# Writing out TensorE's order for the layer change and the second attention: quarters of P times V between score pieces, P turned one unit ahead

## The chip, the cores and the metric

The kernel runs on one core of one Trainium2 chip. The metric is the device time of one execution in microseconds (us), given as the median of several executions. A ratio is the mean time of one kernel's fast runs over the mean time of the other kernel's fast runs of the same rounds, so it is not quite the ratio of the medians that stand beside it. The medians and ranges are over all runs of a kernel, those in the slow state too: one slow run each in e4, e10, e11 and e13, and three in e5. A verdict of faster or slower needs the 95% interval to lie outside 2%.

Two words are used throughout. TensorE is *warm* when its clock runs in full and *cold* when it runs at half rate. The Trainium skill, "TensorE: Matmul & The Clock Gate", Part 1, says that the half rate is the default and that a busy window of about 3.4 us (free-running) releases it. Traces agree on the two states: a score matmul of 512 columns takes 628 ns in one and about 400 ns in the other, with little in between. The clock column of the profile is not always right about the state, so in this text a state is read from those durations.

A *unit* is one key-value head of the attention: scores, softmax, P times V, output projection. There are 8 in each attention.

## The reference, cut to what matters

```python
def _A_ref(x, k_cache, v_cache, wq, wo):          # B=4, 1 query row, 32 heads on 8 kv heads, Dh=128
    W = min(4096, max(256, Sk // 4))              # Sk=8192: the last 2048 keys
    q = (x @ wq).reshape(B, Sq, Hq, Dh).transpose(0, 2, 1, 3)
    k = jnp.repeat(k_cache[:, :, Sk - W:, :], rep, axis=1)
    v = jnp.repeat(v_cache[:, :, Sk - W:, :], rep, axis=1)
    p = _softmax(jnp.einsum("bhqd,bhkd->bhqk", q, k) * (Dh ** -0.5), axis=-1)
    return jnp.einsum("bhqk,bhkd->bhqd", p, v)... @ wo

x = x + _A_ref(_layernorm(x), ...)                # first attention
x = x + _B_ref(_layernorm(x), ...)                # gated MLP
x = x + _A_ref(_layernorm(x), ...)                # second attention, same K, V and weights
x = x + _B_ref(_layernorm(x), ...)
```

## The kernel before

Operations are recorded with what they read and write. A list scheduler with a small time model then fixes the order of each engine, so the source order is only a priority. These are the parts that matter, for one unit.

```python
def softmax_unit(tag, hk):
    q_unit(tag, hk, k2)                                   # "qx" on TensorE, "qe": ACT copies to qbd
    def e_s(pe):                                          # ONE operation of 20 matmuls
        for gi in range(4): pe.matmul(ps[...bank...], msk_s, msk_m..., start=True, stop=False)       # L713, mask
        for cp in range(4):
            for gi in range(4): pe.matmul(ps[...], qbd[...], kt[...], start=False, stop=(cp == 3))   # L720, scores
    P.op("tensor", "S" + tag, ...)
    P.op("vector", "mx" + tag, ...)                       # L728 maximum, then three small steps to nm (L740)
    P.op("scalar", "ex" + tag, ...)                       # L743 exponential

def turn_p(tag, k2):
    P.op("tensor", "pp" + tag, ...)                       # L752 one 128x512 matmul
    P.op("scalar", "pc" + tag, ...)                       # L754 copy
    P.op("vector", "pt" + tag, ...)                       # L757 transpose to ebuf
    ...                                                   # four small POOL steps
    P.op("tensor", "sb" + tag, ...); P.op("vector", "ri" + tag, ...)   # L771, L778: 1/sum

def pv_unit(tag, h, k2, tiles):
    for bp, name in tiles:
        P.op("tensor", "PV...", 32 matmuls, ...)          # L792, twice 32 matmuls
    P.op("vector", "oe" + tag, ...)                       # L800 scaling by 1/sum
    P.op("tensor", "pm" + tag, ...); P.op("vector", "oq" + tag, ...)   # L810, L815

def attn(L):
    for ui in range(2):
        ks[ui] = front(ui); turn_p(ui)                    # front = scores and softmax
    for ui, h in enumerate(hs):
        if ui + 2 < HKV: ks[ui + 2] = front(ui + 2)
        ov = pv_unit(tag, h, ks[ui], v_tiles[(L, h)])
        if ui + 2 < HKV: turn_p(ui + 2)
        wo_unit(tag, h, ov, ...)                          # L831, 16 matmuls
    # ... (cut)

fill(); x_in()
q_proj(0, ...); attn(0); glu(0, 0, NB)
q_proj(1, ...); attn(2); glu(1, 0, NB, True)
```

Of the kernel before, what the change touches and what calls it, by code (L numbers as in the profile page):

```python
# [40 lines left out]
class _Plan:  # L41
    def __init__(self):
        self.ops = []
        self.last_w = {}
        self.readers = {}
        self.bank_eng = {}
        self.bank_cur = {}
        self.bank_prev = {}

    def op(self, eng, name, dur, emit, r=(), w=(), banks=(), dma_bytes=0, dma_rate=0.0, after=(), lazy=0.0):  # L50
# [26 lines left out]
        for t in w:  # L77
            self.last_w[t] = o
            self.readers[t] = []
        deps.discard(o)  # L80
# [168 lines left out]
class _SlotPool:  # L249
# [14 lines left out]
    sem_lat=100.0, pick_tol=60.0,  # L264
    dma_issue=60.0, dma_lat0=900.0, dma_lat1=1100.0, dma_max_out=16,
    bw_8k=430.0, bw_4k=412.0, bw_3k=409.0, bw_1k=356.0,
    pe_pair=38.0, pe_small=230.0, pe_f32=450.0, pe_row=80.0, pe_sq=300.0,
    dve_fix=150.0, dve_f32=1.04, dve_small=90.0,
# [4 lines left out]
def build(nc, A_x, A_k, A_v, A_wq, A_wo, B_wg, B_wu, B_wd, out, cfg=None):  # L273
# [41 lines left out]
    with es:  # L315
# [56 lines left out]
        def tile_ap(s):  # L372
            return arena[:, s * SLOT:(s + 2) * SLOT]
# [42 lines left out]
        def need(name):  # L416
            while name not in where:
                take_load()
            return where[name]
# [53 lines left out]
        def wq_part(k, c, i):  # L473

            if k == 0:
                return ("wq", c, k), i * SLOT
            return ("wq", (i, c // 2), k), (c % 2) * SLOT
# [161 lines left out]
        def q_proj(k, b0, b1, variance):  # L639
            assert b0 == 0 and b1 == NB  # L640
            after = ()
            for n, i in enumerate((0, 1) if k == 0 else (1, 0)):
                qb = OBS[n]
                for c in range(NC):
                    name, o = wq_part(k, c, i)
                    s = need(name)

                    def e_q(pe, c=c, s=s, qb=qb, o=o):
                        last = None
                        for hh in range(4):  # L650
                            last = pe.matmul(ps[32 * hh:32 * hh + NB, qb, :], xn[:, c * NB:(c + 1) * NB],  # L651
                                             tile_ap(s)[:, o + hh * 512:o + (hh + 1) * 512],
                                             start=(c == 0), stop=(c == NC - 1))
                        return last
                    P.op("tensor", "q%d_%d_%d" % (k, i, c), 4 * tm["pe_row"], e_q,
                         r=tok(s) + [("xn",)], w=[("qrow", i)], banks=(qb,), after=after if k else ())
                    done(name)
                if variance is not None:
                    variance()
                    variance = None  # L660
                P.op("vector", "qt%d_%d" % (k, i), c_dve(512),
                     lambda v, qb=qb: v.transpose(  # L662
                         ebuf[:, :], ps[:, qb, :].rearrange("p (x k t) -> p x t k", k=32, t=2)),
                     r=[("qrow", i)], w=[("e", 0), ("e", 1)], banks=(qb,))
                qi = qh[:, i * 64:(i + 1) * 64]
                qc = P.op("vector", "qc%d_%d" % (k, i), c_dve(64),
                     lambda v, qi=qi: v.tensor_tensor(
                         qi.rearrange("p (c b r) -> p c b r", c=4, b=NB),
                         ebuf[:, :].rearrange("p (r c y) -> p c y r", c=4, y=32)[:, :, 0:NB],
                         lnr[:, 0:NB].unsqueeze(1).unsqueeze(3).broadcast_to([128, 4, NB, REP]), ALU.mult),  # L670
                     r=[("e", 0), ("e", 1), ("lnr", 0)], w=[("qh", i)])
                if k and n == 0:
                    fresh.append(qc)
                    after = (qc,)
# [26 lines left out]
        ucount = [0]  # L701

        def softmax_unit(tag, hk):
# [4 lines left out]
            q_unit(tag, hk, k2)  # L708

            def e_s(pe):  # L710
                last = None
                for gi in range(4):
                    last = pe.matmul(ps[32 * gi:32 * gi + 32, bank, :], msk_s[:, :],  # L713
                                     msk_m[:, :].unsqueeze(1).broadcast_to([128, 256, 2]), start=True, stop=False)
                for cp in range(4):
                    for gi in range(4):
                        jh, bp = gi // 2, gi % 2
                        kt = kpair(hk, bp).rearrange("p (j c k t) -> p c t j k", c=2, k=32, t=2)
                        q0 = ((k2 * 4 + cp) * 2 + bp) * 32
                        last = pe.matmul(ps[32 * gi:32 * gi + 32, bank, :], qbd[:, q0:q0 + 32],  # L720
                                         kt[:, cp // 2, cp % 2, jh * NJ:(jh + 1) * NJ, :], start=False, stop=(cp == 3))
                return last
            P.op("tensor", "S" + tag, 20 * tm["pe_row"], e_s,
                 r=[("msk_s",), ("msk_m",)] + [("slot", 4 * hk + t) for t in range(4)] + [("q", k2)],
                 w=[("pss", pt)], banks=(bank,))
# [4 lines left out]
            for g in range(2):  # L730
# [8 lines left out]
            P.op("vector", "nm" + tag, tm["dve_small"],  # L739
                 lambda v: v.tensor_reduce(nmax[:, 2 + k2:3 + k2], mk, AXX, ALU.max, negate=True, apply_transpose=True),  # L740
# [6 lines left out]
            return k2  # L747

        def turn_p(tag, k2):
            ob = OBS[k2]  # L750
# [16 lines left out]

            def e_sb(pe):
                last = None
                for n, sn in enumerate((hi, mid, lo)):  # L770
                    last = pe.matmul(ps[:, ob, 128:128 + NR], sn.broadcast_to([128, 128]), sel_b[:, :],  # L771
                                     start=(n == 0), stop=(n == 2))
                return last
            P.op("tensor", "sb" + tag, 3 * tm["pe_pair"], e_sb,
                 r=[("s3", k2, n) for n in range(3)] + [("sel_b",)], w=[("psb", k2)], banks=(ob,))
            rv = rinv[:, k2 * NR:(k2 + 1) * NR]
            P.op("vector", "ri" + tag, c_dve(NR) + 60.0,
                 lambda v: v.reciprocal(rv, ps[:, ob, 128:128 + NR]),  # L778
                 r=[("psb", k2)], w=[("rinv", k2)], banks=(ob,))

        def pv_unit(tag, h, k2, tiles):
            ob = OBS[k2]
            ev = ebuf[:, k2 * 256:(k2 + 1) * 256].bitcast(BF16).rearrange("p (m x t) -> p t m x", x=32, t=2)
            for bp, name in tiles:
                s = need(name)

                def e_pv(pe, s=s, bp=bp):
                    last = None
                    src = tile_ap(s)
                    for j in range(2 * NJ):  # L790
                        x0 = j // 16 * 16 + bp * 8
                        last = pe.matmul(ps[:, ob, bp * 8:bp * 8 + 8], src[:, j * 128:(j + 1) * 128],  # L792
                                         ev[:, j % 2, j % 16 // 2, x0:x0 + 8], start=(j == 0), stop=(j == 2 * NJ - 1))
                    return last
                P.op("tensor", "PV%s_%d_%d" % (tag, h, bp), 2 * NJ * tm["pe_pair"], e_pv,
                     r=tok(s) + [("e", k2)], w=[("pso", k2, bp)], banks=(ob,))
                done(name)
            ov = onb[:, k2 * NR:(k2 + 1) * NR]
# [5 lines left out]
                 r=[("pso", k2, bp) for bp in range(2)] + [("rinv", k2)], w=[("on", k2)], banks=(ob,))  # L804
            op = onp[:, k2 * REP * NR:(k2 + 1) * REP * NR]
# [34 lines left out]
        def attn(L):  # L840
            hs = list(range(HKV)) if L == 0 else list(range(HKV))[::-1]

            def front(ui):
                h = hs[ui]
                if L == 0:
                    k_transpose(h)
                k2 = softmax_unit("%d.%d" % (L, ui), h)
                if L == 2:
                    for bp in range(2):
                        pool.release(4 * h + 2 * bp)  # L850
                    fill()
                return k2

            ks = {}
            for ui in range(2):
                ks[ui] = front(ui)
                turn_p("%d.%d" % (L, ui), ks[ui])
            for ui, h in enumerate(hs):
                tag = "%d.%d" % (L, ui)
                if ui + 2 < HKV:  # L860
                    ks[ui + 2] = front(ui + 2)
                if L == 0 and ui == HKV - 1:
                    stash(stashed)
                ov = pv_unit(tag, h, ks[ui], v_tiles[(L, h)])
                if ui + 2 < HKV:
                    turn_p("%d.%d" % (L, ui + 2), ks[ui + 2])
                wo_unit(tag, h, ov, ks[ui], ui == 0, ui == HKV - 1)
# [154 lines left out]
        q_proj(0, 0, NB, layer_norm("A", 0, NB, True))  # L1022
        attn(0)
        glu(0, 0, NB)
        q_proj(1, 0, NB, layer_norm("Q", 0, NB, True))
        attn(2)
# [70 lines left out]
```

## Time and profile before

| | before |
|---|---|
| time, median of 3 (range) | 188.27 us (188.03 to 188.72) |
| span in the profiled run | 186.5 us |
| bytes by DMA, end of the last load | 71.84 MB, about 178.9 us |
| first P times V of the second attention | 137.05 us |
| last output projection of the second attention ends | 175.47 us |
| from there to the end of the span | 11.0 us |

The span in 40 slices: each digit is the busy share of a slice in tenths, PEclk is the granted clock.

```profile
## 2 busy tenths in 40 slices
PE   1434433764716465352855473358778988995694
PEclk9999999999999999999999999999987555576558
DMA  5999999999999999999999999999899999999910
```

The DMA row is full until 177 us. The chain that ended last, as shares of the span, says the same: mostly memory stream.

```profile
DMA 47%; PE 25%; DVE 13%; SPq 6%; ACT 4%; issue 4%; ACTq 0%
```

The turn of P (L752) is missing among the matmuls of the timeline, and only its weight loads have a record:

```profile
157.27 0.10 PEld L752 LDWEIGHTS ps<-prow,perm 128*128 128x128 bf16 x1 [0.32 <-ACT prow L743]
162.87 0.10 PEld L752 LDWEIGHTS ps<-prow,perm 128*128 128x128 bf16 x1
```

The exponentials' line from the groups of 115 to 185 us (busy, mean ns, idle before, releasers) is the symptom that the change aims at:

```profile
L743 ACT ACTIVATE prow<-ps,nmax 128x512 bf16<-128x512 f32 x8 | 5.5, 688 | 18.7 <-DVE onb L800 12.8 <-DVE nmax L740 5.1 <-DVE ebuf L757 0.8
```

### The profile page before, as it was taken

To read this page: it belongs to the slowest core of one execution; us is meant where nothing else is said; L and a number is where in the kernel's file an instruction comes from. 1 tells how busy PE (TensorE), PEld (TensorE's weight loads), DVE (VectorE), ACT (ScalarE), POOL (GpSimd) and SP (SyncE) were. 2 spreads that over 40 slices of the span, in tenths; PEclk is the share of its full clock that TensorE was granted. 3 is DMA by queue.
4 is the path that set the end of the run, shared out by engine and by line. 5 is a ranking of instruction groups with operands and counts; after the bars stand their busy time and mean duration, and the time that the engine had idled before them with its cause. 6 is when DMAs were issued, how large, how long until landed. Compare 5 with 4: busy or idle time off the path is not lost.

```text
span 186.5 us, 4596 instructions
## 1 busy us (share of the span) xinstructions
PE 109.6 (59%) x2018; PEld 65.5 (35%) x2032; DVE 93.4 (50%) x240; ACT 31.1 (17%) x78; POOL 15.8 (9%) x85
## 2 busy tenths in 40 slices
PE   1434433764716465352855473358778988995694
PEld 1002111342403333141444431312255655655532
DVE  4209999376583737639242543216754413442241
ACT  2002003230212103020020010001263213212010
POOL 7000001110100001010010000000031111012000
PEclk9999999999999999999999999999987555576558
DMA  5999999999999999999999999999899999999910
GB/s 196 422 427 427 422 416 417 417 420 418 413 427 417 422 422 411 427 424 413 419 417 417 399 403 419 334 375 420 353 411 427 425 418 417 416 403 406 378 55 1
DMA packets 12307, 72.12 MB, mean 387 GB/s; under 512 B 1144, under 2 KB 1152, under 8 KB 5632
## 3 DMA queue, kind: packets, MB, share of 16 engines
q1 hardware_dynamic: 12280, 71.84, 94.4%
q8 instruction: 15, 0.25, 0.5%
q14 instruction: 4, 0.03, 0.0%
q10 hardware_dynamic: 8, 0.00, 0.0%
HBM read 71.83 MB, written 0.00 MB: 385 GB/s over the span
## 4 chain that ended last, share of the span: by engine, by line
DMA 47%; PE 25%; DVE 13%; SPq 6%; ACT 4%; issue 4%; ACTq 0%
DMA arena<-in_A_v_cache_dram 23%; DMA arena<-in_A_k_cache_dram 14%; PE ps L720 9%; SPq L387 6%; DMA arena<-in_A_wq_dram 5%; DMA arena<-in_B_w_up_dram 5%; PE ps L792 4%; DVE arena L698 3%; PE ps L713 3%; ACT prow L743 3%; PE ps L893 2%; DVE nmax L728 2%; PE ps L651 2%; DVE ps L496 1%; PE ps L831 1%
## 5 line engine op out<-in xcount | busy, mean ns | idle before, releaser
L792 PE MATMUL ps<-ebuf,arena 128*128 128x8 bf16 x1024 | 32.0, 168 | 23.1 <-DMA arena<-in_A_v_cache_dram 17.2
L792 PEld LDWEIGHTS ps<-ebuf,arena 128*128 128x128 bf16 x1024 | 29.9, 103 | 25.7 <-DMA arena<-in_A_v_cache_dram 22.1
L698 DVE STREAM_TRANSPOSE arena<-arena 128x1024 f32<-128x1024 f32 x32 | 37.9, 1213 | 1.1 <-DMA arena<-in_A_k_cache_dram 1.0
L720 PE MATMUL ps<-arena,qbd 128*32 128x512 bf16 x256 | 29.2, 595 | 0.0
L728 DVE TENSOR_REDUCE nmax<-ps 128x1 f32<-128x512 f32 x16 | 11.0, 687 | 26.1 <-PE ps L720 26.0
L713 PE MATMUL ps<-msk_m,msk_s 128*32 128x512 bf16 x64 | 10.1, 583 | 15.6 <-DVE arena L698 13.2
L743 ACT ACTIVATE prow<-ps,nmax 128x512 bf16<-128x512 f32 x16 | 11.0, 687 | 49.4 <-DVE nmax L740 25.1
L761 POOL CAST s<-psm 128x1 bf16<-128x1 f32 x16 | 3.0, 186 | 147.8 <-ACT prow L743 147.8
L651 PE MATMUL ps<-arena,xn 128*4 128x512 bf16 x64 | 8.4, 606 | 8.9 <-DMA arena<-in_A_wq_dram 7.8
L720 PEld LDWEIGHTS ps<-arena,qbd 128*32 128x32 bf16 x256 | 9.1, 132 | 12.2 <-issue 11.3
L691 ACT CAST qbd<-ps 128x256 bf16<-128x256 f32 x16 | 5.9, 371 | 38.1 <-PE ps L720 30.7
L754 ACT CAST prow<-ps 128x512 bf16<-128x512 f32 x16 | 9.4, 586 | 10.5 <-PE ps L810 3.2
L831 PE MATMUL ps<-onp,arena 128*128 128x16 bf16 x256 | 9.2, 174 | 3.0 <-DVE onp L815 3.0
L757 DVE STREAM_TRANSPOSE ebuf<-prow 128x256 f32<-128x256 f32 x16 | 6.9, 431 | 6.4 <-ACT prow L754 6.3
L800 DVE TENSOR_TENSOR onb<-ps,rinv 128x16 bf16<-128x16 f32 x16 | 2.8, 174 | 13.8 <-PE ps L792 13.8
L662 DVE STREAM_TRANSPOSE ebuf<-ps 128x512 f32<-128x512 f32 x4 | 2.9, 717 | 13.5 <-PE ps L651 13.4
L831 PEld LDWEIGHTS ps<-onp,arena 128*128 128x128 bf16 x256 | 8.0, 103 | 4.0 <-DVE onp L815 2.0
L628 ACT ACTIVATE lnv<-ps 128x4 f32<-128x4 f32 x4 | 0.7, 174 | 49.7 <-PE ps L624 49.7
L686 PE MATMUL ps<-qh,eyew 32*128 32x64 bf16 x64 | 5.9, 226 | 5.0 <-ACT qbd L691 1.9
L893 PE MATMUL ps<-arena,xn 128*4 128x448 bf16 x64 | 6.8, 564 | 2.4 <-DMA arena<-in_B_w_up_dram 1.7
L713 PEld LDWEIGHTS ps<-msk_m,msk_s 128*32 128x32 bf16 x64 | 1.9, 100 | 17.0 <-DVE arena L698 10.1
L810 PE MATMUL ps<-onb,permo 128*128 128x16 bf16 x64 | 4.3, 178 | 3.6 <-DVE onb L800 3.6
(75 smaller groups left out, 92.7 us busy)
## 6 DMA issues: line engine op xcount, KB each, us to landing
arena<-in_A_v_cache_dram SPq DMA_DIRECT2D x30, 1024.0 KB, 20.6
arena<-in_A_k_cache_dram SPq DMA_DIRECT2D x16, 1024.0 KB, 25.1
arena<-in_A_wq_dram SPq DMA_DIRECT2D x8, 1024.0 KB, 9.5
arena<-in_A_wo_dram SPq DMA_DIRECT2D x4, 1024.0 KB, 25.2
arena<-in_B_w_gate_dram SPq DMA_DIRECT2D x4, 896.0 KB, 17.7
arena<-in_B_w_up_dram SPq DMA_DIRECT2D x4, 896.0 KB, 15.9
arena<-in_B_w_down_dram SPq DMA_DIRECT2D x2, 1024.0 KB, 12.8
arena<-in_B_w_down_dram SPq DMA_DIRECT2D x1, 768.0 KB, 7.4
```

The source lines that it names most:

```text
L387: o = P.op("sync", name, 0.0, lambda e, dst=dst, src=src: e.dma_start(dst, src), r=r, w=w, dma_bytes=nbytes, dma_rate=tm[rate])
L651: last = pe.matmul(ps[32 * hh:32 * hh + NB, qb, :], xn[:, c * NB:(c + 1) * NB], tile_ap(s)[:, o + hh * 512:o + (hh + 1) * 512], start=(c = ...
L698: P.op("vector", "T%d_%d" % (h, t), c_dve(1024), lambda v, v32=v32: v.transpose(v32, v32), r=[("slot", 4 * h + t)], w=[("slot", 4 * h + t)])
L713: last = pe.matmul(ps[32 * gi:32 * gi + 32, bank, :], msk_s[:, :], msk_m[:, :].unsqueeze(1).broadcast_to([128, 256, 2]), start=True, stop= ...
L720: last = pe.matmul(ps[32 * gi:32 * gi + 32, bank, :], qbd[:, q0:q0 + 32], kt[:, cp // 2, cp % 2, jh * NJ:(jh + 1) * NJ, :], start=False, s ...
L728: lambda v: v.tensor_reduce(nmax[:, k2:k2 + 1], ps[:, bank, :], AXX, ALU.max),
L743: lambda a: a.activation(prow[:, :].rearrange("p (m x t) -> p m x t", x=32, t=2), ps[:, bank, :].rearrange("p (m t x) -> p m x t", x=32, t ...
L754: P.op("scalar", "pc" + tag, c_act(512), lambda a: a.copy(prow[:, :], ps[:, PBS[k2], :]), r=[("ppb", k2)], w=[("prow",)], banks=(PBS[k2],))
L757: lambda v: v.transpose(ebuf[:, k2 * 256:(k2 + 1) * 256], prow[:, :].bitcast(F32)),
L792: last = pe.matmul(ps[:, ob, bp * 8:bp * 8 + 8], src[:, j * 128:(j + 1) * 128], ev[:, j % 2, j % 16 // 2, x0:x0 + 8], start=(j == 0), stop ...
L831: last = pe.matmul(ps[:, WB, c * NR:(c + 1) * NR], tile_ap(s)[:, o + r_ * D + c * 128:o + r_ * D + (c + 1) * 128], ov[:, r_ * NR:(r_ + 1) ...
L893: last = pe.matmul(ps[32 * g:32 * g + NB, OBS[n], 0:NF], xn[:, c * NB:(c + 1) * NB], tile_ap(s)[:, o:o + NF], start=(c == 0), stop=(c == N ...
```

## The change

The intent is to break the loop of latencies. TensorE's order is no longer left to the scheduler from the second query projection to the end of the second attention: every TensorE operation depends on the one before it (`P.chain`). The score block of unit u+2 is split into five pieces, mask and four score pieces, which stand between quarters of unit u's P times V. P of unit u+1 is turned in the middle of unit u. Four 512-column matmuls a unit (`filler`) are added, meant to keep the clock up. A quarter of the second query projection (two of its eight groups of four matmuls) moves behind the first two score blocks. Constants of the scheduler's time model change too. The core of the diff:

```diff
+        if eng == "tensor":
+            if self.chain:
+                deps.add(self.last_t)
+            self.last_t = o
...
-        def softmax_unit(tag, hk):
+        def score_pieces(tag, hk):
+            def piece(cps, last):          # cps: (-1,) the mask, (0,) to (3,) four score matmuls each
...
+        def filler(k2):
+            def e_f(pe):
+                for g in range(4):
+                    last = pe.matmul(ps[32 * g:32 * g + 32, PBS[k2], :], permo[:, 32 * g:32 * g + 32], permo[:, :], start=True, stop=True)
...
+        def attn_second():
+            for u in range(2):
+                q_unit(tag(u), hs[u], u)
+                sp, soft_late = score_pieces(tag(u), hs[u])
+                sp((-1, 0, 1, 2, 3), u == 0)
+                free(u)
+            q_rest((nms[tag(0)],))
+            q_unit(tag(2), hs[2], 0)
+            turn_a(tag(0), 0)
+            turn_b(tag(0), 0)
+            soft_late()
+            for u in range(HKV):
...
+                pv(0)
+                score(-1)
+                score(0)
+                if u == HKV - 1:
+                    op[u - 1] = o_turn(tag(u - 1), 1 - k2)
+                pv(1)
+                if u < HKV - 1:
+                    project()              # output projection of unit u-1
+                score(1)
+                pv(2)
+                if u == HKV - 1:
+                    project()
+                else:
+                    turn_a(tag(u + 1), 1 - k2)
+                score(2)
+                pv(3)
+                o_even(tag(u), k2)         # scaling by 1/sum, on DVE
+                score(3)
+                if more:
+                    free(u + 2)
+                if u + 3 < HKV:
+                    q_unit(tag(u + 3), hs[u + 3], 1 - k2)
+                if u + 1 < HKV:
+                    turn_b(tag(u + 1), 1 - k2)
+                for n in range(cfg.get("FILL", 1) if more else 0):
+                    filler(k2)
+                if u != HKV - 2:
+                    op[u] = o_turn(tag(u), k2)
...
+        P.chain = True
+        q_second(layer_norm("Q", 0, NB, True))
+        attn_second()
+        P.chain = False
```

## The prediction

> **What bounds the kernel now.** Two things, in turn. The slice rows show the 16 DMA engines at 9 tenths or more from 5 to 177 us (71.84 MB, about 420 GB/s): the memory stream sets the pace. The last load lands near 178 us, but the span ends at 186.5: in the timeline the second attention's last output projection ends at 175.5 us, and the last layer then runs 11.0 us on weights that are mostly there.
>
> Why the second attention is late, by the chain of waits, 150 to 169 us: a unit takes about 5.6 us (maxima start at 154.76, 160.19, 165.79) and is one serial loop: mask and scores 2.35, maximum to negated maximum 1.9, exponential 0.8, its sum read 0.2, queue 0.3 to 0.6. P's turn stands before the next scores in TensorE's queue, so they wait for the exponential. TensorE is also cold: the windows view grants 0.50 from 146 to 165.5 us; a score matmul takes 628 ns there against 381 to 400 at 132 to 134 us, and 20 of them 2.15 us against 1.2 to 1.5. The Trainium skill, "TensorE: Matmul & The Clock Gate", Part 1, describes a half-rate state left only after a busy free-running window of about 3.4 us; the flips at 138.3, 141.7 and 165.5 us fit. (From 20 to 110 us that column says 1.00, yet score matmuls take 628 ns: durations count.)
>
> **What the change does.** No byte and no large operation is removed. The loop is cut: score pieces of unit u+2 stand between quarters of unit u's P times V (32 matmuls take 0.96 us, a quarter about half), and P of unit u+1 is turned mid-unit. Added: six fillers of four 512-column matmuls (0.22 us warm, 0.43 cold each). Half of the second query block follows the first two score blocks; P times V, which started at 137.05, should start near 134.5.
>
> **A unit after** (estimates from these durations): TensorE warm 1.8 PV + 1.1 scores + 0.45 projection + 0.9 small ones + 0.2 filler, about 4.5; cold 5.9 to 6.5. The remaining latency loop is about 4.4. V arrives at 5.0 us per unit, the last near 165 us. So warm, attention follows the DMA and ends at 168 to 171 us instead of 175.5; cold, nothing is won.
>
> **What of it counts.** The last 0.26 MB still lands about 177.5 to 178 us (the queue's dip at 131 to 134 us, 0.7 us, may shrink: K slots are freed earlier). After it come 0.3 us of matmuls, 0.45 copy, 1.8 output DMA: span about 181 at best, 182.5 to 183 timed. I expect attention to end near 170.5 and some cold windows to remain.
>
> **Predicted: 183.6 us, range 181.8 to 187.0 (8 in 10). Faster by over 2%: 0.62; within 2%: 0.33; slower: 0.05.**
>
> **What would show it.** Maxima about 5.0 us apart; the exponential's wait on DVE (12.8 us after 115 us) mostly gone; clock mostly 1.00 from 135 to 165 us with short score matmuls; P times V waiting for V's DMA in later units; attention over by 171 us; the last down weights' DMA in the chain's end.
>
> **What would make it wrong.** Interleaving spreads the score bursts, so no window is busy enough and the clock stays at 0.50: units take 6 us and the time stays near 188. Weight switches may cost idle time 8 times a unit. A fixed TensorE order turns a late softmax into a stall of everything. Later slot releases could starve the DMA queue.

## More of the kernel before

Where the attention begins, the timeline shows something else that turned out to matter. Three score blocks (L720) are done before the first P times V (L792), and two of them are warm:

```profile
128.12 1.92 PE L720 MATMUL ps<-arena,qbd 128*32 128x512 bf16 x16
...
131.53 1.14 PE L720 MATMUL ps<-arena,qbd 128*32 128x512 bf16 x16
...
133.58 1.11 PE L720 MATMUL ps<-arena,qbd 128*32 128x512 bf16 x16
...
137.05 0.96 PE L792 MATMUL ps<-ebuf,arena 128*128 128x8 bf16 x32
```

The timeline of TensorE (start, duration, operation, in brackets the idle time before it) shows one cold unit of the second attention, from mask to mask:

```profile
157.82 0.62 PE L713 MATMUL ps<-msk_m,msk_s 128*32 128x512 bf16 x4 [0.77 <-ACT qbd L691]
158.22 1.92 PE L720 MATMUL ps<-arena,qbd 128*32 128x512 bf16 x16
160.07 0.25 PE L771 MATMUL ps<-sel_b,s 128*128 128x16 bf16 x3
160.17 0.57 PE L831 MATMUL ps<-onp,arena 128*128 128x16 bf16 x16
160.60 0.99 PE L792 MATMUL ps<-ebuf,arena 128*128 128x8 bf16 x32
161.53 0.39 PE L686 MATMUL ps<-qh,eyew 32*128 32x64 bf16 x4
161.85 1.01 PE L792 MATMUL ps<-ebuf,arena 128*128 128x8 bf16 x32
162.72 0.25 PE L810 MATMUL ps<-onb,permo 128*128 128x16 bf16 x4
163.41 0.62 PE L713 MATMUL ps<-msk_m,msk_s 128*32 128x512 bf16 x4 [0.44 <-ACT qbd L691]
```

A unit takes 163.41 − 157.82 = 5.59 us. It looks as if TensorE rests for 0.77 us before the first mask and 0.44 us before the second, but most of that is misread.

## The result

The change made the kernel slower: 196.81 us median (196.07 to 197.88, 4 runs) against 188.25 us (188.03 to 188.72, 4 runs) beside it. The ratio is 1.0456, 95% interval 1.0393 to 1.0518. The prediction of 183.6 us, range 181.8 to 187.0, was wrong in size and in sign.

Line numbers move with the change: mask L713 → L734, scores L720 → L740, P times V L792 → L830, projection L831 → L876, turn of P L752 → L782, exponential L743 → L771; the filler is L889.

The slices and the chain after the change:

```profile
PE   1452515837434272432866734586999999997695
PEclk9999999999999999999999999999999999999999
DMA  6999999999999999999999999999999999991000
PE 48%; DVE 27%; DMA 13%; issue 4%; ACT 4%; SPq 1%; another core or an unknown queue 0%; ACTq 0%; DVEq 0%
```

DMA moved the same 71.84 MB and finished at about 178.2 us, 0.7 us earlier than before. It no longer has the last word: PE now leads the chain with 48%, and TensorE's row is at 9 for the eight slices from 137 to 176 us. The clock row says full speed everywhere. It is not to be believed, as the durations of one unit show:

```profile
150.04 0.62 PE L734 MATMUL ps<-msk_m,msk_s 128*32 128x512 bf16 x4
150.44 0.64 PE L740 MATMUL ps<-arena,qbd 128*32 128x512 bf16 x4
151.02 0.59 PE L830 MATMUL ps<-ebuf,arena 128*128 128x8 bf16 x16
151.46 0.57 PE L876 MATMUL ps<-onp,arena 128*128 128x16 bf16 x16
151.97 0.62 PE L740 MATMUL ps<-arena,qbd 128*32 128x512 bf16 x4
152.52 0.59 PE L830 MATMUL ps<-ebuf,arena 128*128 128x8 bf16 x16
153.48 0.62 PE L740 MATMUL ps<-arena,qbd 128*32 128x512 bf16 x4 [0.38 <-issue]
154.03 0.59 PE L830 MATMUL ps<-ebuf,arena 128*128 128x8 bf16 x16
154.55 0.62 PE L740 MATMUL ps<-arena,qbd 128*32 128x512 bf16 x4
155.10 0.39 PE L704 MATMUL ps<-qh,eyew 32*128 32x64 bf16 x4
155.42 0.25 PE L804 MATMUL ps<-sel_b,s 128*128 128x16 bf16 x3
155.60 0.62 PE L889 MATMUL ps<-permo 128*32 128x512 bf16 x4
156.15 0.27 PE L855 MATMUL ps<-onb,permo 128*128 128x16 bf16 x4
156.28 0.57 PE L830 MATMUL ps<-ebuf,arena 128*128 128x8 bf16 x16
156.77 0.62 PE L734 MATMUL ps<-msk_m,msk_s 128*32 128x512 bf16 x4
```

This unit takes 156.77 − 150.04 = 6.73 us, and TensorE works through all of it. (The 0.38 us at 153.48 is again the turn of P, whose matmul has no record; its weight load stands at 152.94.) Every 512-column group is at its cold length. The latency loop no longer holds TensorE up: from 137 to 176 us no gap before a recorded matmul is put down to another engine. On the side of ACT, the previous output scaling (L800 before) is no longer named as what the exponentials wait for:

```profile
L771 ACT ACTIVATE prow<-ps,nmax 128x512 bf16<-128x512 f32 x8 | 5.5, 688 | 9.2 <-DVE nmax L768 9.2
```

Before, that group waited 12.8 + 5.1 = 17.9 us for DVE (releasers are inferred), so the wait was halved. But TensorE now bounds the unit with more work than before, 6.73 against 5.59 us.

The start of the attention lacks one of the three early score blocks, and both that are left are cold:

```profile
128.49 1.92 PE L740 MATMUL ps<-arena,qbd 128*32 128x512 bf16 x16
...
131.60 1.92 PE L740 MATMUL ps<-arena,qbd 128*32 128x512 bf16 x16
...
136.49 0.59 PE L830 MATMUL ps<-ebuf,arena 128*128 128x8 bf16 x16 [0.27 <-DVE ebuf L787]
```

From the first P times V to the end of the last projection the kernel before needs 175.47 − 137.05 = 38.4 us and the changed one 183.85 − 136.49 = 47.4 us, 9 us more. An estimate from the unit costs that the experiments below measure: fillers 6 × 0.64 = 3.8, the finer alternation 6 × 0.48 = 2.9, and one whole block of mask and scores (0.40 + 1.85 = 2.25) moved from before that stretch into it, together about 9.0 us. In this sum the warm stretches of the kernel before and its own waits are taken to cancel.

A further 1.1 us is lost behind the attention: from the last projection to the end of the span it takes 196.0 − 183.85 = 12.1 us, against 11.0 before. The last down projection, the same 28 matmuls, runs cold:

```profile
182.39 1.87 PE L951 MATMUL ps<-arena,hT 128*4 128x256 bf16 x28 [0.63 <-DVE hT L920]
190.40 3.15 PE L1066 MATMUL ps<-arena,hT 128*4 128x256 bf16 x28 [0.25 <-DVE hT L1035]
```

The first line is the kernel before, the second the changed one.

### The profile page after: what moved, and what is told of

It is laid out like the page before. It is cut to its first block, busy times and chain, and to the rows that moved or that the text cites. A ratio compares the mean times of both kernels' runs of the same rounds, so it can differ in the third digit from the quotient of the medians.

```text
span 196.0 us, 4648 instructions
## 1 busy us (share of the span) xinstructions
PE 119.7 (61%) x2041; PEld 67.5 (34%) x2056; DVE 95.0 (48%) x240; ACT 31.7 (16%) x78; POOL 16.0 (8%) x85
## 3 DMA queue, kind: packets, MB, share of 16 engines
q1 hardware_dynamic: 12280, 71.84, 90.0%
## 4 chain that ended last, share of the span: by engine, by line
PE 48%; DVE 27%; DMA 13%; issue 4%; ACT 4%; SPq 1%; another core or an unknown queue 0%; ACTq 0%; DVEq 0%
PE ps L740 15%; DVE arena L716 14%; PE ps L830 12%; DMA arena<-in_A_wq_dram 10%; PE ps L734 5%; PE ps L876 4%; DMA arena<-in_B_w_down_dram 3%; DVE nmax L756 3%; PE ps L855 2%; PE ps L1066 2%; ACT prow L771 2%; ACT prow L784 2%; DVE nmax L760 1%; PE ps L889 1%; PE ps L704 1%
## 5 line engine op out<-in xcount | busy, mean ns | idle before, releaser
L716 DVE STREAM_TRANSPOSE arena<-arena 128x1024 f32<-128x1024 f32 x32 | 36.9, 1203 | 0.0
L830 PEld LDWEIGHTS ps<-ebuf,arena 128*128 128x128 bf16 x1024 | 30.6, 104 | 17.3 <-issue 15.1
L740 PE MATMUL ps<-arena,qbd 128*32 128x512 bf16 x256 | 34.2, 624 | 2.3 <-issue 2.3
L830 PE MATMUL ps<-ebuf,arena 128*128 128x8 bf16 x1024 | 33.8, 168 | 2.5 <-DMA arena<-in_A_v_cache_dram 1.7
L734 PE MATMUL ps<-msk_m,msk_s 128*32 128x512 bf16 x64 | 9.9, 608 | 23.3 <-DVE arena L716 22.4
L771 ACT ACTIVATE prow<-ps,nmax 128x512 bf16<-128x512 f32 x16 | 11.0, 688 | 36.9 <-DVE nmax L768 36.9
L740 PEld LDWEIGHTS ps<-arena,qbd 128*32 128x32 bf16 x256 | 8.7, 125 | 10.9 <-issue 10.7
L804 PE MATMUL ps<-sel_b,s 128*128 128x16 bf16 x48 | 3.9, 177 | 12.9 <-ACT prow L784 12.9
L876 PE MATMUL ps<-onp,arena 128*128 128x16 bf16 x256 | 9.3, 174 | 3.4 <-DVE onp L860 3.2
L734 PEld LDWEIGHTS ps<-msk_m,msk_s 128*32 128x32 bf16 x64 | 1.8, 100 | 24.4 <-DVE arena L716 19.4
L876 PEld LDWEIGHTS ps<-onp,arena 128*128 128x128 bf16 x256 | 8.1, 104 | 4.2 <-DVE onp L860 2.3
L842 DVE TENSOR_TENSOR onb<-ps,rinv 128x16 bf16<-128x16 f32 x16 | 3.1, 191 | 12.1 <-PE ps L830 12.0
L664 DVE STREAM_TRANSPOSE ebuf<-ps 128x512 f32<-128x512 f32 x3 | 2.2, 717 | 12.4 <-PE ps L653 12.3
```

The lines of the kernel that those rows point to most:

```text
L716: P.op("vector", "T%d_%d" % (h, t), c_dve(1024), lambda v, v32=v32: v.transpose(v32, v32), r=[("slot", 4 * h + t)], w=[("slot", 4 * h + t)])
L734: ins = pe.matmul(ps[32 * gi:32 * gi + 32, bank, :], msk_s[:, :], msk_m[:, :].unsqueeze(1).broadcast_to([128, 256, 2]), start=True, stop=F ...
L740: ins = pe.matmul(ps[32 * gi:32 * gi + 32, bank, :], qbd[:, q0:q0 + 32], kt[:, cp // 2, cp % 2, jh * NJ:(jh + 1) * NJ, :], start=False, st ...
L771: lambda a: a.activation(prow[:, :].rearrange("p (m x t) -> p m x t", x=32, t=2), ps[:, bank, :].rearrange("p (m t x) -> p m x t", x=32, t ...
L830: last = pe.matmul(ps[:, ob, bp * 8:bp * 8 + 8], src[:, j * 128:(j + 1) * 128], ev[:, j % 2, j % 16 // 2, x0:x0 + 8], start=(j == 0), stop ...
L876: last = pe.matmul(ps[:, WB, c * NR:(c + 1) * NR], tile_ap(s)[:, o + r_ * D + c * 128:o + r_ * D + (c + 1) * 128], ov[:, r_ * NR:(r_ + 1) ...
```

## The experiments

Fifteen kernels were run, all with correct results. Each was timed in 3 rounds beside the kernel before.

| kernel | median us (range) | before | ratio, 95% interval |
|---|---|---|---|
| e1_nofill | 193.47 (192.83 to 195.02) | 189.11 | 1.0236, 1.0176 to 1.0295 |
| e2_warm | 191.65 (190.74 to 192.05) | 189.11 | 1.0120, 1.0074 to 1.0167 |
| e3_block | 195.06 (194.55 to 195.36) | 189.11 | 1.0301, 1.0251 to 1.0351 |
| e5_warm_block | 194.25 (190.91 to 195.73) | 189.11 | none: three of four runs slow |
| e4_warm_fill3 | 193.08 (191.30 to 197.94) | 189.94 | 1.0148, 1.0064 to 1.0231 |
| e7_block_nofill | 194.44 (193.51 to 196.26) | 189.94 | 1.0263, 1.0187 to 1.0338 |
| e8_before_warm | 186.83 (186.06 to 187.53) | 189.94 | 0.9848, 0.9788 to 0.9909 |
| e9_warm_block_fill | 194.67 (192.24 to 195.01) | 189.94 | 1.0235, 1.0157 to 1.0313 |
| e11_block_oe | 191.65 (189.55 to 192.95) | 189.41 | 1.0073, 0.9980 to 1.0165 |
| e10_before_warm_tail | 187.14 (186.15 to 189.45) | 189.41 | 0.9869, 0.9811 to 0.9928 |
| e12_warm_block_oe_tail | 189.13 (188.98 to 189.30) | 189.41 | 0.9992, 0.9951 to 1.0033 |
| e13_block_late | 192.69 (191.08 to 194.76) | 188.26 | 1.0204, 1.0132 to 1.0275 |
| e14_early | 192.39 (190.42 to 192.78) | 189.05 | 1.0141, 1.0058 to 1.0224 |
| e15_early_warm | 189.37 (187.85 to 189.72) | 189.05 | 1.0001, 0.9935 to 1.0066 |
| e16_before_late | 189.18 (188.06 to 190.71) | 189.05 | 1.0011, 0.9937 to 1.0086 |

The quoted expectations name theories by letters. The first one was that the clock stays cold, that TensorE's cold work then bounds each unit, and that the change added work there. Against it stood that the alternation keeps the clock down and that a block of scores, or a warm start, would bring the predicted gain. Where a quoted letter matters, the text below says which claim was at stake. The diffs are cut: conditions for the first and last units are partly left out, and each is against the kernel that the text names.

### The fillers: e1_nofill

```diff
-                for n in range(cfg.get("FILL", 1) if more else 0):
+                for n in range(cfg.get("FILL", 0) if more else 0):
```

> The changed kernel without its six fillers, nothing else. Theory A (TensorE is saturated by cold matmuls in the second attention; the fillers fail to warm it): each filler block costs 0.55 us of a 6.73 us unit, six of them 3.3 us, so about 193.5 us and still cold (512-column matmuls 600 ns or more in the units). Rival B (the fixed order makes TensorE wait for softmax, the work itself does not matter): the filler only fills waiting time, so 196 to 197 us again.

Measured: 193.47 us. The unit is 6.09 us (masks at 149.10, 155.18, 161.27, 167.36) without idle time on TensorE. The six fillers cost 6.73 − 6.09 = 0.64 us each, 3.8 us in all by the trace. The ratio to the kernel before falls from 1.0456 to 1.0236, about 4.1 us; the medians differ by 3.3 us. They were run at other times. As theory A had it, they bought nothing: the clock was cold with them. (Without them the profiled run was warm from about 134.6 to 138.3 us, but it also began its attention 0.8 us later; its units are as cold.)

### The clock: e2_warm and e4_warm_fill3

Twelve blocks of four 512-column matmuls are put into the waits of the second query phase.

```diff
+        def warm(n, bank):                 # n times four 512-column matmuls into an unused bank
...
-            q_mms(1, 1, OBS[0], range(NC))
+            q_mms(1, 1, OBS[0], (0, 1))
+            warm(4, WB)
+            q_mms(1, 1, OBS[0], (2, 3))
             variance()
             fresh.append(q_turn(1, 1, OBS[0], ebuf[:, :], [("e", 0), ("e", 1)]))
+            warm(2, WB)
             q_mms(1, 0, OBS[1], (0, 1))
+            warm(1, WB)
...                                         # one more after each of the first two q_unit, three before turn_b(tag(0))
```

> The changed kernel with twelve more filler blocks, all before the first P times V, most of them where TensorE waits for the query weights, the query copy or the softmax anyway; the eight units are untouched. Theory A: a dense stretch of over 7 us brings the full clock before the units start; if an interleaved unit is dense enough to hold a clock that it cannot raise, units take 4.5 to 5.0 us, score matmuls about 400 ns, and the time is 182 to 184 us. If the units cannot even hold it, cold sets in within two windows and the time is 194 to 197 us. Rival B: the clock is a side show, units stay above 6 us with waits on ACT or DVE ahead of TensorE even where matmuls are short; over 190 us.

The same unit as in the changed kernel, now warm and then cold:

```profile
140.65 0.40 PE L747 MATMUL ps<-msk_m,msk_s 128*32 128x512 bf16 x4
...
145.65 0.40 PE L747 MATMUL ps<-msk_m,msk_s 128*32 128x512 bf16 x4
...
147.10 0.40 PE L753 MATMUL ps<-arena,qbd 128*32 128x512 bf16 x4
147.43 0.56 PE L843 MATMUL ps<-ebuf,arena 128*128 128x8 bf16 x16
147.85 0.59 PE L795 MATMUL ps<-prow,perm 128*128 128x512 bf16 x1
148.37 0.62 PE L753 MATMUL ps<-arena,qbd 128*32 128x512 bf16 x4
```

A warm unit takes 145.65 − 140.65 = 5.00 us, a cold one again 6.73 (151.67 to 158.40). The clock fell at 147.85 with no idle time before it: these units do not hold full speed although TensorE is recorded busy throughout. Theory A's 182 to 184 us if the clock were held was not reached, since it was not held; the time was 191.65 us. Its other branch, cold within two windows and 194 to 197 us, missed as well: the clock held for about 17 us.

e4_warm_fill3 adds two more fillers to each unit of e2_warm.

> Interleaved, dense stretch in front, and three filler blocks a unit in place of one. Dense stretch alone: units of 4.97 us while warm, dropped to cold at 147.8 us, then 6.73 us. Theory A2 (the clock falls because an interleaved unit, about a third of whose time is streaming, is below a holding threshold): two more blocks a unit (0.33 us each warm) hold it through the last scored unit; units about 5.6 us and no 600 ns score matmul before 170 us; 185 to 187.5 us. Rival C (the clock falls for another reason, for example after a fixed time at full rate): it falls near 148 us again, cold units are then 7.8 us, time 196 us or more.

The units stayed warm until about 156.5 us (5.41 us from mask to mask at 139.69, 145.10 and 150.51) and turned cold some 2 us after a gap of 0.72 us within P times V that the trace gives to "issue". A cold unit then cost 7.58 us. The time was 193.08 us with a wide range, no gain over e2_warm; both stated figures, 185 to 187.5 and 196 us or more, missed. More fillers hold the clock longer, but while they hold it they cost 0.41 us a unit (5.41 − 5.00), and after it is lost 0.85 (7.58 − 6.73).

### The alternation: e3_block, e7_block_nofill, e11_block_oe

e3_block does the scores as one block again, still with the filler. Against the changed kernel:

```diff
                 pv(0)
-                score(-1)
-                score(0)
...
                 pv(1)
                 project()
-                score(1)
                 pv(2)
                 turn_a(tag(u + 1), 1 - k2)
-                score(2)
+                sp((-1, 0, 1, 2, 3), True)
                 pv(3)
                 o_even(tag(u), k2)
-                score(3)
```

> The changed kernel with the interleaving alone undone: the 20 score matmuls of a unit stand in one block after P's turn; fixed order, early softmax and fillers stay. Theory A with bursts: no weight switches between quarters (about 0.12 us each, seven a unit, 5 us in all), and a score block plus P's turn of 2.6 us dense work can fill a 3.4 us window and raise the clock in some units: 186 to 191 us, with short score matmuls in some units. Rival B (fixed order): same as the changed kernel, 195 to 197 us.

Measured: 195.06 us, far from 186 to 191 and inside the rival's 195 to 197. e7_block_nofill is the same without fillers.

> Fixed order and early softmax alone: scores in one block, no filler. Theory D (the units of the kernel before were already bound by cold TensorE work, about 5.4 of their 5.5 us, so cutting the latency loop is worth nothing): the unit is 5.6 to 5.9 us cold, time 188.5 to 191 us. Rival (the prediction's: the units of before were bound by the serial loop, with about 0.7 us of TensorE idle in it): the unit is 4.9 to 5.1 us even cold, and the time is 184 to 186.5 us.

Measured: 194.44 us. The unit is 6.45 us in both. In e7 0.75 us of it is TensorE waiting for the output scaling (`o_even`), so the work is 6.45 − 0.75 = 5.70 us. In the block order the scaling stands on DVE behind the maximum chain of the score block; the alternation had hidden that. In e3_block the filler stands in that wait. So a new wait replaced the saving, and both expectations missed it.

e11_block_oe moves the fourth quarter and the scaling ahead of the turn and the scores (against e7_block_nofill):

```diff
-                    turn_a(tag(u + 1), 1 - k2)
-                if more:
-                    sp((-1, 0, 1, 2, 3), True)
                 pv(3)
                 o_even(tag(u), k2)
+                if more:
+                    turn_a(tag(u + 1), 1 - k2)
+                    sp((-1, 0, 1, 2, 3), True)
```

> Fixed order and early softmax, scores in one block, no filler, and the block moved behind the last quarter so that the output's scaling goes ahead of the next maximum on DVE. The earlier block version without filler waited 0.75 us a unit for that scaling: 6.45 us. Theory D (TensorE's cold work bounds the unit and it is the same work as in the kernel before, 5.59 us): the unit is 5.6 to 5.8 us and the time 188 to 191 us. Rival (cutting the serial loop is worth something once nothing else waits): 5.3 us or less and under 187 us.

Measured: 191.65 us (189.55 to 192.95), just outside both of theory D's figures and far from the rival's. A cold unit is 6.06 us with a smaller wait, now for the step after the scaling:

```profile
160.12 0.60 PE L876 MATMUL ps<-onp,arena 128*128 128x16 bf16 x16 [0.45 <-DVE onp L860]
...
161.94 0.62 PE L734 MATMUL ps<-msk_m,msk_s 128*32 128x512 bf16 x4
162.34 1.92 PE L740 MATMUL ps<-arena,qbd 128*32 128x512 bf16 x16
```

Work alone is 6.06 − 0.45 = 5.61 us, the 5.59 us of the kernel before. (Two stretches of this run, about 142.3 to 145.6 and 152.3 to 155.7 us, were warm and three of its units shorter, 5.35 to 5.77 us. So its time gains from the clock as well as from the order.) So the alternation costs 6.09 − 5.61 = 0.48 us a unit on TensorE: in e1_nofill the four score pieces take 0.58 + 0.55 + 0.55 + 0.55 = 2.23 us from start to start of what follows, and 1.85 us as one block; the projection takes 0.51 between pieces and 0.43 elsewhere. The alternating unit has six more changes between 32-column and 128-column weights than the block, so one costs about 0.08 us (an estimate, 0.48 / 6). The Trainium skill, "TensorEngine Tiling (Array Packing)", Key Properties, says that changing the tiling mode drains TensorE; a cost at each change agrees with that, and its size is what these runs add. In the time the block order shows no such gain: with its wait of 0.45 us a cold unit is only 6.09 − 6.06 = 0.03 us shorter than the alternating one.

### Both together: e5_warm_block, e9_warm_block_fill, e12_warm_block_oe_tail

e5 is e2_warm with e3_block. e9 adds three more fillers a unit to it: FILL 3, and one filler after the second quarter. e12 is e11_block_oe with the warm-up and four filler blocks in the tail after the attention.

> Score block and the dense stretch together. Theory A: if interleaving matters only through the clock and the switches, this is at least as fast as the dense stretch alone minus its switches, 182 to 184 us if the clock holds; if blocks leave windows of pure P times V that drop the clock, it is 185 to 190 us and slower than the interleaved kernel with the dense stretch. Rival B: over 190 us.

> Fixed order, scores in a block, dense stretch, and four filler blocks a unit, three of them where the warm block version waits 0.6 to 0.75 us for the output's scaling anyway. Theory A2: the clock holds to the end of the last scored unit, units 4.8 to 5.3 us, near the 5.0 us that V's DMA needs; 182 to 185 us, faster than both kernels. If the clock is not held: cold units of 7.5 us or more, 196 us or more.

> The same two sets of fillers on the fixed order with score blocks and no filler in the units. Theory A with D: units about 4.5 us while warm and 5.6 to 5.8 us cold, the clock lost within two units of the start: 185 to 188 us, within 1% of the kernel before with the same fillers. If the fixed order is worth something by itself once the clock is equal: 183 us or less.

e5: its profiled run, 190.91 us, was the only fast one. e9 came to 194.67 us: warm until about 141 us, then 6.78 us a unit. In each of these units the scores are cold (1.92 us) while the three fillers behind them are warm (0.83 us), so the clock rose and fell once a unit; its expectation missed. e12 came to 189.13 us, level with the kernel before (0.9992), and missed its 185 to 188 us. It was warm until about 135.3 us and its cold units are the 6.06 us of e11_block_oe. Beside it ran e10_before_warm_tail, the kernel before with two similar sets of fillers (below; seven and four against twelve and four): at 187.14 us it is 2 us faster. So with the clock helped on both sides the order written by hand is still the slower one. In the block order, too, full speed was not held in these runs.

### The projection later, and one more score block early: e13_block_late, e14_early

e13_block_late puts the projection behind the third quarter, so that its operand is ready (against e11_block_oe):

```diff
                 pv(1)
-                if u < HKV - 1:
-                    project()
                 pv(2)
+                project()
```

> The last block version with the output projection moved behind the third quarter, so that its 0.45 us wait a unit goes. Nothing is left but the fixed order, the early softmax and the cut loop: same matmuls as the kernel before, no filler, no interleaving. Theory D: with no wait left, the unit is the cold TensorE work, 5.59 to 5.65 us, no shorter than before's, and the time is 188 to 190 us. Rival (the loop was the binding one before by a margin): units of 5.3 us or less, under 187 us. If some other wait appears in its place, units stay near 6.0 us.

Measured: 192.69 us, no better than e11_block_oe, and the expectation of 188 to 190 us missed. The unit fell to 5.88 us, but this includes 0.28 us of "issue" in P times V in place of the wait, and the trace has two more such gaps of 0.94 and 0.99 us. The profiled run was a slow one (194.76 us), so only its unit structure is read here.

By now a unit had the work of the kernel before, and still 192.69 − 188.26 = 4.4 us were lost in this version. Theory F: the loss is the score block that the kernel before does ahead of its first P times V. e14_early scores unit 2 there and runs the scores three units ahead (against e13_block_late):

```diff
+            sp, soft_next = score_pieces(tag(2), hs[2])
+            sp((-1, 0, 1, 2, 3), False)
+            free(2)
+            q_unit(tag(3), hs[3], 1)
...
-                    sp((-1, 0, 1, 2, 3), True)
+                    soft_next()
+                    sp, soft_next = score_pieces(tag(u + 3), hs[u + 3])
+                    sp((-1, 0, 1, 2, 3), False)
```

> e13_block_late with a third score block scored ahead of the first probability turn, so that scores run three units ahead of P times V, as the kernel before has it; no fillers. Theory F (what e13_block_late still loses to the kernel before is the one score block less that is done in TensorE's wait for the first exponential, some 2.3 us of cold TensorE work): 190 to 191 us, the first P times V still starts at about 137, the cold units stay at 5.6 us of work, the last unit's projection ends about 2 us earlier than in e13_block_late against the first P times V. Rival (the rest is the clock and unexplained gaps): 192 to 193 us, no change outside the interval.

Measured: 192.39 us. This is the rival's number, and the intervals of e13 and e14 overlap; theory F alone falls. The trace says why:

```profile
135.90 1.92 PE L740 MATMUL ps<-arena,qbd 128*32 128x512 bf16 x16
...
139.84 1.87 PE L830 MATMUL ps<-ebuf,arena 128*128 128x8 bf16 x64 [0.17 <-DVE ebuf L787]
```

The third block is cold, and the first P times V starts at 139.84 instead of about 137. The block was moved into time that was not free. In the kernel before the same three blocks cost little because the second and third were warm, from 131.53 us on.

### The same, warm: e15_early_warm

> e14_early with the warm-up blocks in the second query phase. If both theories hold (one more score block early, and full clock for the stretch until about 140): 187 to 189 us, 2 to 3 us less than e14_early. Rival (the warm-up only delays the query phase, since full clock is lost at once when the block-ordered units start): within 1 us of e14_early.

This is e14_early with the nine warm-up blocks that e2_warm has in the query phase and after the first two `q_unit` (without its three at the turn). Measured: 189.37 us (187.85 to 189.72), against 192.39 us (190.42 to 192.78) for e14_early, so the ranges do not touch, and ratio 1.0001 to the kernel before. The blocks before the first P times V:

```profile
132.78 1.08 PE L753 MATMUL ps<-arena,qbd 128*32 128x512 bf16 x16
...
135.89 1.76 PE L843 MATMUL ps<-ebuf,arena 128*128 128x8 bf16 x64 [0.50 <-DVE ebuf L800]
```

P times V starts 139.84 − 135.89 = 3.95 us earlier than in e14_early, and the last projection ends at 174.83 us instead of 180.11, where e14_early has lost 2.09 us to an "issue" gap near the end. From 138 us on, most units are cold again: the score blocks at 143.2, 153.5 and 159.3 us last 1.92 us. So the clock during the query phase and the first scores is worth 3 us of time, and with it the hand-written order does as well as the scheduler's order without a warm-up.

### The kernel before, warmed: e8_before_warm, e10_before_warm_tail, and the control e16_before_late

If the clock before the first P times V is worth that much, the kernel before should gain from it too. e8 puts seven warm-up blocks into its second query projection, pinned by dependencies:

```diff
+                    if k and c == 1:
+                        after = after + (warm((4, 1)[n], lq),)
                 if variance is not None:
                     variance()
                     variance = None
+                    if k:
+                        warmed = warm(2, [o for o in P.ops if o.eng == "tensor"][-1])
...
-                    after = (qc,)
+                    after = (qc, warmed)
```

> The kernel before with seven filler blocks in front of and between its query matmuls, nothing else. Theory A: the full clock comes some 3 to 6 us earlier but is lost again by 142 us as before, since nothing holds it: within 1% of before, 187 to 189 us. Rival: the clock, once raised early, holds through the units of the kernel before (its scores stand in blocks), units 4.9 us, 184 us or less.

Measured: 186.83 us (186.06 to 187.53), ratio 0.9848. This is the fastest kernel; it beats the kernel before by 1.5%, which the interval separates from nothing but not from 2%. It is 10 us below the changed one, and its expectation, within 1%, missed. All its score blocks before the first P times V are warm (1.08 to 1.13 us). Its last projection ends at 173.41 us against 175.47.

e10_before_warm_tail adds four filler blocks to the tail, to make the last down projection warm.

> The kernel before with the seven filler blocks ahead of its units and four more in the waits around the last output projection and the last layer norm. Theory A: the tail from the last projection to the last down matmuls becomes dense enough for one whole window, so the 28 down matmuls take 1.7 to 1.9 us in place of 3.15 us; 185 to 186.5 us. If the clock stays cold there: 187 to 187.5 us, the fillers costing 0.3 us.

The down projection's matmuls did fall from 3.15 us in e8 to 1.69 (in e16_before_late, below, they took 1.69 without any filler there), but the time, 187.14 us, is that of e8, and the expected 185 to 186.5 us missed. This is left at that: the saving, if there is one, is below what these runs resolve.

One thing was not clean in e8. The scheduler reacted to the seven blocks and also changed the order around the first P times V, so that the scores of units 2 and 3 both stand before it. e16_before_late takes nearly that order in the kernel before, without any warm-up block:

```diff
-                 w=[("pss", pt)], banks=(bank,))
+                 w=[("pss", pt)], banks=(bank,), after=tuple(o for o in P.ops if tag == "2.2" and o.name == "pp2.0"))
```

> The kernel before with the score block of unit 2 pinned behind the first probability turn, without fillers: the scheduler then gives almost the order that e8_before_warm has around the first P times V. A control for e8_before_warm. If e8_before_warm gained by the clock: 188.5 to 190.5 us here, no gain. If it gained by that changed order: 186 to 187.5 us here too.

Measured: 189.18 us, ratio 1.0011 (0.9937 to 1.0086). The order alone gives nothing, so the gain of e8 is the clock's, as far as a control that is close to e8's order, but not identical to it, can say. The profiled run of e16 also lost 4.8 us to three "issue" gaps (1.32, 1.52 and 1.98 us), against 2.8 us in the two longest of e8, which blurs the comparison further.

## Why the prediction was wrong, point by point

**"cold, nothing is won".** This is the step that failed most. The prediction had a cold unit of the new order at 5.9 to 6.5 us, against the 5.6 us before, and called that no gain. Measured were 6.73 us, 1.14 us a unit more than before: 0.64 of it the filler (estimated at 0.43; e1_nofill) and 0.48 to 0.50 the switches between weights of different width (e1_nofill against e11_block_oe), which were named as a risk and put at nothing in the sum although the skill's page says that such a change drains TensorE. Even the prediction's own range meant a loss of 2 to 5 us over six units, which was not carried into the odds: slower by over 2% got 0.05.

**"clock mostly 1.00 from 135 to 165 us with short score matmuls".** In the profiled run it was cold all through: 607 to 634 ns in every recorded score, mask and filler matmul of the second attention (the turns have no record). The prediction's first item under what would make it wrong came true for the clock; the time that it gave for this case, near 188 us, did not. The fillers neither started nor held full speed, and warm units (5.00 us in e2_warm, against the predicted 4.5) lost it after about 17 us.

**The serial loop as the bound.** The loop of 5.6 us was there, and it was cut: the exponentials' wait on DVE fell from 17.9 to 9.2 us. But it was not the only bound. TensorE's cold work was about 5.6 us as well (5.59 in the unit shown, 5.61 in e11_block_oe less its wait), and most of the slack read before each mask was a matmul without a record. Breaking one of two nearly equal bounds gains next to nothing: e7, e11 and e13 have the loop cut and no filler, and their cold units stay at 5.88 us or more. The shortest one of all, with every wait gone, is 5.43 us in e14_early (masks at 142.09 and 147.52), only 0.16 us below the kernel before; the rival expected 5.3 or less.

**"P times V … should start near 134.5".** It started at 136.49 us. The turn of P stands behind the rest of the query projection and one more `qx` in the fixed order, then waits for an ACT copy. And the comparison left out the third score block that the kernel before had done by then.

**What was not in the prediction at all.** The kernel before is warm from 131.3 to 138.3 us, and its query projections and first scores stand close together there: 5.40 us busy of the 6 from 126 to 132 us, and 5.93 in e16_before_late, which also turns warm at 131 us. The changed order has 4.79 there, and e13 and e14 have 4.40 and 4.45, and all three stay cold in this stretch. But density in such a window does not decide it alone. From 128 to 134 us the changed kernel is busy for 5.45 us and stays cold; e1_nofill, with the same order up to its first P times V, is busy for 5.08 and is warm from about 134.6 us. The same code even seems to come out both ways. In every trace here the clock column stays at 1.00 until full speed is first lost and follows the durations from there, so a run whose mean clock is 1.00 never lost it; in the profiled one that is because it was never warm. Of the four runs of the changed kernel two have a mean of 1.00 (197.46 and 197.88 us) and two of 0.87 (196.16 and 196.07): the latter were probably warm for a while, and are about 1.6 us faster. That the clock in this stretch is worth about 3 us is tested, both ways round (e15_early_warm, e8_before_warm).

**What was right.** The DMA stream is not hurt (last load at about 178.2 us), the latency loop is cut, and a fixed order turned late operands into waits as feared, though only in the block variants.

So the profiled span, 9.5 us longer, comes apart as follows (an estimate from the traces): the fillers 3.8 us, the alternation 2.9, the third score block moved into the stretch 2.25 less the 0.56 us by which that stretch begins earlier, and the cold down projection 1.1. Of these the fillers are confirmed by the time: removing them takes 2.2 points off the ratio (1.0456 to 1.0236), one point being about 1.9 us. The alternation is not: its 0.48 us is read from the units. The ratio does fall by 1.6 points from e1_nofill to e11_block_oe, but their cold units differ by 0.03 us, e11_block_oe had warm stretches, and e13_block_late, also without alternation, is back at 1.0204. The cold start is worth 1.4 points (e14_early to e15_early_warm). With the fillers and the alternation gone and the start warmed, e12 and e15 are level with the kernel before; no order written by hand beat it.

Open: what makes the gaps of 0.7 to 2.1 us inside a single operation that the traces give to "issue" (1.23 us from 170.84 us in the kernel before, 2.09 us until 176.57 in e14_early, 1.03 us in e8_before_warm); what exactly counts as activity for the clock, and why the same order is warm at its start in one run and cold in another; and why e5_warm_block had one fast run in four. No run tests the changed constants of the scheduler's time model by themselves; up to the second attention the traces leave them little room, as the third of the four groups of eight query matmuls starts at 126.28 us, against 126.89 before.

## What to carry to other kernels

Before cutting a latency loop, add up the start-to-start times of everything on the engine in one turn of the loop, at the clock that the durations show, and look for records that are missing: if that sum equals the loop, the cut gains nothing and every instruction added is paid in full. A filler for the clock belongs where the engine waits anyway; the same four 512-column matmuls cost 0.64 us each time in a saturated loop, and a few of them won 3 us in the waits of the query phase. Keep operations that use weights of the same width together, and when an order is written by hand, compare also what the scheduler had done *before* the loop began.

## What the Trainium skill lacked or had wrong

- "TensorE: Matmul & The Clock Gate", Part 1 ("HAM oscillation"), gives the rule of no TensorE idle gaps above about 3.4 us. It is not sufficient. From 121 to 184 us the changed kernel has no gap above 1.66 us, and from 137 to 176 us it is recorded busy (with matmul ends that the profiler models) except for the 0.38 us a unit of the missing turn; its score, mask and filler matmuls took 607 to 634 ns throughout. In e2_warm full speed was lost at 147.85 us with no gap at all. A figure for the activity that a window needs, and for what counts as activity when 8-column matmuls stand between 512-column ones, is lacking.
- The same part warns that trace events of the clock can be unreliable. The clock column read 1.00 over the whole profiled run of the changed kernel, at cold durations. In every trace here it reads 1.00, cold or warm, until full speed is first lost, and fits the durations from there (0.50 from 148 us on in e2_warm). Durations decide.
- "TensorEngine Tiling (Array Packing)", Key Properties, says that a change of tiling mode drains TensorE and gives no time for it. Here six more changes between 32-column and 128-column weights cost 0.48 us, about 0.08 us each, cold: four score pieces take 2.23 us against 1.85 as a block.
- No page found warns that a matmul's record can be missing while its weight load is recorded, and that it then reads as idle time (0.44 us before the mask at 163.41 us in the kernel before, 0.38 us a unit in the changed one).
- No page found explains the gaps of 0.7 to 2.1 us inside one operation that nothing in the trace releases.
